# Transposes of k and q as row halves side by side, one exp per pair of heads, and a new order at both ends of the attention stage

## The chip, the cores and the metric

The kernel runs on one core of one Trainium2 chip. The metric is device time in microseconds (us), lower is better. PE is TensorE (its weight loads are listed as PEld), DVE is VectorE, ACT is ScalarE, POOL is GpSimd, SP is SyncE, which issues nearly all DMAs of this kernel.

## The reference

Attention with a soft cap on the scores, then two feed-forward stages on the 896 tokens that it gives:

```python
# q, k, v: (2, 12, 448, 64) f32, cap = 30
scores = cap * tanh(q @ k.T / sqrt(64) / cap)
attn = softmax(scores) @ v                       # then heads side by side: x (896, 768)
h = x @ w_in                                     # (896, 1024)
solu = h * softmax(h)
x = layer_norm(solu) * g_ln @ w_out              # (896, 768)
g, val = x @ w_gate, x @ w_val                   # (896, 1536) each
return (silu(g) * val) @ w_out2                  # (896, 768)
```

The weights arrive as 64-bit floats and are turned into f32 on the chip.

## The kernel before, in words

**Precision.** Every large product is made of three matmuls in the type float32r: a tensor is split into a high part (`hi_act`, `hi_dve`: a rounding copy on ACT or DVE) and a low part (`lo_dve`: the difference, on DVE), and hi·hi, hi·lo and lo·hi are added up in PSUM.

**Attention.** The 24 heads go two at a time, as 12 pairs; pair i has the tiles `k_i`, `q_i` and `v_i`. `attn_load` brings each of them with two DMAs, one per head: 448 rows of 64 numbers, laid out as 112 partitions that hold four consecutive rows each. `attn_T` transposes k and q of a pair on PE, 4 + 4 transposes of 112 rows x 128 columns into the PSUM tile `T` (tag `t`, two banks), and splits the result into `ks` (high part on ACT, for pair 1 on DVE; low part on DVE). `attn_qk(i, c)` makes chunk c of the scores, with 112 keys on the partitions: six matmuls into the PSUM tile `sc`, of which there are two (`psc`, bufs=2), head 0 from partitions 0 to 63 and head 1 from 64 to 127; ACT then takes the tanh of both heads (112x896) into `P`. `attn_exp` is an exp over two chunks at once (112x1792), so there are two per pair. `attn_sums` adds `P` up over the keys with matmuls against ones (tile `S`); DVE transposes the sums, POOL copies pieces of them, and `attn_recip` makes the reciprocals. `attn_pv` is the product with v (tile `pv`); `attn_norm` scales it and splits it into x.

**Order.** `attn_pair(i)` writes out the order by hand, and `InOrder` keeps it on each engine: while scores of pair i are made, k and q of pair i+1 are transposed, and sums, `pv` and norm of pair i-1 are done. `w_steps[i]` are four pieces of the conversion of `w_in` (tiles `wi`), which fill DVE. The 13th call, `attn_pair(12)`, has only the rest of pair 11 left, and takes three of the six steps of `h` for the first 128 tokens (`fill`) ahead of it; each step is six matmuls of 512 columns. `keep_warm(n)` issues n matmuls of zeros, 64x64, whose result nobody reads.

**After attention** the scheduler places instructions: h for seven blocks of 128 tokens, its softmax and layer norm, transposes (`lt`), x2, the gated stage and `ff2_out`, which writes 14 blocks of 128 x 384 results.

**Order of tokens.** Because a partition holds four consecutive rows of q, chunk c of a transposed q holds the rows 4p + c. The tokens stay in that order through both feed-forward stages, and `ff2_out` puts them right when it writes: each block goes out in two parts, the larger from SP's queue, the other from ACT's.

The functions that the diff touches, and what calls them:

Of the kernel before, what the change touches and what calls it, by code (L numbers as in the profile page):

```python
# [5 lines left out]
F32 = mybir.dt.float32  # L6
# [3 lines left out]
AF = mybir.ActivationFunctionType  # L10
# [26 lines left out]
class Kernel:  # L37
# [142 lines left out]
    def attn_load(self, i, names="kqv"):  # L180

        nc, CP = self.nc, self.CP
        b, p = divmod(i, self.NP)
        r = self.raws.setdefault(i, {})
        for n in names:
            src, bufs = {"k": (self.k, 2), "q": (self.q, 2), "v": (self.v, 3)}[n]
            r[n] = t = self.raw.tile([CP, 512], F32, name=f"{n}_{i}", tag=n, bufs=bufs)
            for j in range(2):
                sj = src[b, 2 * p + j].rearrange("(p c) d -> p c d", c=4)
                nc.sync.dma_start(t.rearrange("p (c h d) -> p c h d", c=4, h=2)[:, :, j, :], sj)  # L190

    def attn_T(self, i):

        CP, S = self.CP, self.S
        r = self.raws[i]
        ks = r["ks"] = self.at.tile([128, 2, 2, S], F32R, name=f"ks_{i}", tag="ks", bufs=2)
        ps = self.pt.tile([128, 2, 512], F32, name=f"T_{i}", tag="t")
        lots = ("k", "q") if i == 0 else ("kq",)
        for names in lots:
            for n in names:  # L200
                m = "kq".index(n)
                for c in range(4):
                    self.transpose(ps[:, m, c * CP:(c + 1) * CP], r[n][:, c * 128:(c + 1) * 128], self.ident[:CP, :CP])
            m = slice("kq".index(names[0]), "kq".index(names[-1]) + 1)
            (self.hi_dve if i == 1 else self.hi_act)(ks[:, m, 0], ps[:, m, :S])
            self.lo_dve(ks[:, m, 1], ps[:, m, :S], ks[:, m, 0])

    def attn_qk(self, i, c):


        CP, S = self.CP, self.S
        r = self.raws[i]
        ks = r["ks"]
        if c % 2 == 0:
            r["P", c // 2] = self.at.tile([CP, 2, 2, S], F32, name=f"P_{i}_{c}", tag="P", bufs=4)
        sc = self.psc.tile([128, 2, 512], F32, name=f"sc_{i}_{c}", tag="sc")
        for n, (u, w) in enumerate(((0, 0), (0, 1), (1, 0))):
            for j in range(2):
                h = slice(64 * j, 64 * j + 64)
                self.PE.matmul(sc[:CP, j, :S], ks[h, 0, u, c * CP:(c + 1) * CP], ks[h, 1, w, :], start=n == 0, stop=n == 2)  # L220
        self.A.activation(r["P", c // 2][:, c % 2], sc[:CP, :, :S], AF.Tanh, scale=self.c1[:CP])

    def attn_exp(self, i, g):


        P = self.raws[i]["P", g]
        self.A.activation(P, P, AF.Exp, scale=self.cp[:self.CP])

    def attn_sums(self, i):


        S = self.S
        r = self.raws[i]
        ps = self.pt.tile([128, 512], F32, name=f"S_{i}", tag="S")
        for m in range(2):
            for g in range(4):
                self.PE.matmul(ps[32 * g:32 * g + 32, :S], self.ones, r["P", m][:, g % 2, g // 2, :], start=m == 0,
                               stop=m == 1, tile_position=(0, 32 * g))
        tr = r["r"] = self.at.tile([128, S], F32, name=f"tr_{i}", tag="rc", bufs=2)
        sm = r["sm"] = self.at.tile([128, 32], F32, name=f"sm_{i}", tag="sm", bufs=2)[:, :S // 32]  # L240
        self.V.transpose(tr, ps[:, :S])
        for g in range(4):
            a, z = slice(32 * g, 32 * g + 32), slice(32 * (g ^ 1), 32 * (g ^ 1) + 32)
            self.G.tensor_copy(sm[a], tr[z, ::32])
# [9 lines left out]
    def attn_pv(self, i, c):  # L254

        S = self.S
        r = self.raws[i]
        if c == 0:
            r["pv"] = self.pt.tile([128, 512], F32, name=f"pv_{i}", tag="pv", bufs=1)
        for g in range(4):  # L260
            o = c * 128 + 32 * g
            self.PE.matmul(r["pv"][32 * g:32 * g + 32, :S], r["v"][:, o:o + 32], r["P", c // 2][:, c % 2, g // 2, :],
                           start=(c == 0), stop=(c == 3), tile_position=(0, 32 * g))

    def attn_norm(self, i):
# [10 lines left out]
    def attn_pair(self, i, fill=()):  # L276


        last, n = i - 1, 2 * self.NP
        if i == 0:  # L280
            self.attn_load(2, "v")
            self.w_in_load(1)
        elif i + 2 < n:
            self.attn_load(i + 2)
        w = self.w_steps[i]

        early = i > 1
        w[0]()
        if i < n:
            self.attn_qk(i, 0)  # L290
            self.attn_qk(i, 1)
        if i + 1 < n:
            self.attn_T(i + 1)
        if i < n:
            self.attn_exp(i, 0)
            if early:
                self.attn_qk(i, 2)
                self.attn_qk(i, 3)
        for f in fill:
            f()  # L300
        if i:
            self.attn_sums(last)
        w[1]()
        w[2]()
        if i:
            self.attn_pv(last, 0)
            self.attn_pv(last, 1)
            self.attn_recip(last)
        w[3]()
        if i < n:  # L310
            if not early:
                self.attn_qk(i, 2)
                self.attn_qk(i, 3)
            self.attn_exp(i, 1)
        if i:
            self.attn_pv(last, 2)
            self.attn_pv(last, 3)
            self.attn_norm(last)
# [174 lines left out]
            self.lo_dve(d[:, 1, :], f[:, m], d[:, 0, :])  # L493

    def ff2_out(self, half, t):
        nc, S, CP = self.nc, self.S, self.CP
        N = self.DM // 2
        acc = self.pt.tile([128, 512], F32, name=f"o_{half}_{t}", tag="m")[:, :N]
        for fc in range(self.K2):
            a, w = self.a[fc], self.w2[half, fc]  # L500
            c = slice(t * 128, (t + 1) * 128)
            self.mm3(acc, (a[:, 0, c], a[:, 1, c]), (w[:, 0, :], w[:, 1, :]), fc == 0, fc == self.K2 - 1)
        ob = self.slot("e", [128, N], f"ob_{half}_{t}", F32, bufs=2)
        nc.scalar.activation(ob, acc, AF.Copy)  # L504
        ov = self.out.rearrange("(b p c) e -> b c p e", b=self.B, c=4)
        r, parts = 0, []
        while r < 128:
            b, m = divmod(t * 128 + r, S)
            cc, p0 = divmod(m, CP)
            n = min(128 - r, CP - p0)  # L510
            parts.append((n, ov[b, cc, p0:p0 + n, half * N:(half + 1) * N], ob[r:r + n, :]))
            r += n
        for m, (_, dst, src) in enumerate(sorted(parts, key=lambda v: -v[0])):
            (nc.scalar if m else nc.sync).dma_start(dst, src)


    def run(self):
        nc = self.nc
# [6 lines left out]
        self.at = self.pool("at", side="right")  # L525
        psc = self.psc = self.pool("psc", bufs=2, space=PSUM)
        ptA = self.pt = self.ph = self.pool("ptA", bufs=1, space=PSUM)
        self.attn_load(0, "kq")
        self.setup()
        self.attn_load(1, "kq")  # L530
        self.wi = [self.slot(f"wi{u}", [128, KD, F1], f"wi{u}") for u in range(2)]
# [3 lines left out]
        w = [self.w_in_steps(i) for i in range(2 * KD)]  # L535
        none = lambda: None
        w = [(none,) * 4] + w + [(none,) * 4]
        self.w_steps = [(w[i][1], w[i][2], w[i + 1][0], w[i][3]) for i in range(2 * KD + 1)]
        self.attn_T(0)
        self.keep_warm(4)  # L540
        self.attn_load(0, "v")
        self.attn_load(2, "kq")
        self.w_in_load(0)
        self.attn_load(1, "v")
        nc.sync.dma_start(self.gt, self.g_ln.rearrange("(f p) -> p f", p=128))
        h = [self.ff1_h(t) for t in range(7)]
        for i in range(2 * self.NP):
            self.attn_pair(i)
        self.htag = "t"
        self.attn_pair(2 * self.NP, [f for _, f in h[0][:3]])  # L550
        for _, f in h[0][3:]:
            f()
        self.in_order = False
        self.at.release()
# [110 lines left out]
```

## Time and profile before

| | us |
|---|---|
| median of 3 runs | 503.4 (503.26 to 503.74) |
| the profiled execution, its own time | 504.33 |
| span in its profile, first to last instruction | 502.0 |
| PE busy | 492.1 (98%) |
| DVE busy | 351.9 (70%) |
| ACT busy | 251.1 (50%) |

The span is what the trace shows; the 2.3 us between it and the profiled execution's own time lie outside the instructions. The shares are means over stages that differ: attention takes the first 117 us of the span, and there ACT and DVE are far busier than their shares say.

### The profile page before, as it was taken

What the parts mean: (1) busy time and instruction counts of PE and PEld (TensorE: products, weight loads), DVE (VectorE), ACT (ScalarE), POOL (GpSimd) and SP (SyncE); (2) the same over time, 40 slices, a digit from 0 to 9 for tenths busy, and PEclk for the clock granted to TensorE, in tenths of its full rate; (3) what the DMA queues carried; (4) which work ended last, traced back from release to release, by engine and by line L of the source; (5) the groups of instructions that cost most, each with busy time, mean ns of one, the idle gap of its engine ahead of it and who ended that gap; (6) DMA issues with size and microseconds to landing.
All of it is one profiled execution on the core that took longest, in us unless ns stands there. A gap on an engine that the chain in (4) does not pass through costs nothing.

```text
span 502.0 us, 7647 instructions
## 1 busy us (share of the span) xinstructions
PE 492.1 (98%) x3016; PEld 406.1 (81%) x3016; DVE 351.9 (70%) x633; ACT 251.1 (50%) x373; POOL 21.9 (4%) x62
## 2 busy tenths in 40 slices
PE   7899999999999999999999999999999999999996
PEld 6454545456788899898899998889999989999996
DVE  2689999984778894769899999788997867200000
ACT  4999999961224695666544454444434434100000
POOL 1112121210000010000000000000000000000000
PEclk9899999999999999999999999999999999999999
DMA  6856564311000222243535445446344525111111
GB/s 146 218 130 165 129 164 117 103 44 42 1 0 23 76 73 85 85 146 128 185 127 164 151 144 172 125 127 188 96 126 104 179 64 157 33 33 31 33 31 31
DMA packets 66916, 52.40 MB, mean 104 GB/s; under 512 B 35904, under 2 KB 62272, under 8 KB 66880
## 3 DMA queue, kind: packets, MB, share of 16 engines
q1 hardware_dynamic: 66112, 51.13, 35.3%
q10 hardware_dynamic: 736, 0.79, 0.4%
q8 instruction: 23, 0.38, 0.3%
q14 instruction: 13, 0.11, 0.1%
q0 software_dynamic: 32, 0.00, 0.0%
HBM read 49.16 MB, written 2.75 MB: 103 GB/s over the span
## 4 chain that ended last, share of the span: by engine, by line
PE 94%; ACT 3%; DVE 2%; issue 0%; POOL 0%; POOLq 0%
PE o L29 17%; PE g L29 17%; PE v L29 17%; PE x L29 11%; PE h L29 10%; PE pv L29 7%; PE sc L29 6%; PE S L29 4%; PE T L29 2%; ACT P L29 2%; PE lt L29 1%; DVE sm L29 1%; PE warm L29 1%; DVE e L29 0%; ACT e L29 0%
## 5 line engine op out<-in xcount | busy, mean ns | idle before, releaser
L29 PE MATMUL g<-x,y 128*128 128x512 f32 (+1 forms) x432 | 91.2, 363 | 0.0
L29 PE MATMUL v<-x,y 128*128 128x512 f32 (+1 forms) x432 | 90.5, 362 | 0.0
L29 PEld LDWEIGHTS g<-x,y 128*128 128x128 f32 x432 | 78.5, 188 | 8.9
L29 PEld LDWEIGHTS v<-x,y 128*128 128x128 f32 x432 | 78.2, 188 | 8.5
L29 PE MATMUL h<-wi,x 128*128 128x512 f32 x252 | 58.9, 392 | 0.0
L29 PEld LDWEIGHTS h<-wi,x 128*128 128x128 f32 x252 | 46.9, 188 | 11.0 <-issue 1.5
L29 PE MATMUL o<-x,a 128*128 128x384 f32 x294 | 52.3, 334 | 0.0
L29 PEld LDWEIGHTS o<-x,a 128*128 128x128 f32 x294 | 51.1, 188 | 0.0
L29 ACT ACTIVATE P<-sc,consts 112x896 f32<-112x896 f32 x48 | 45.8, 1009 | 5.7 <-PE sc L29 5.7
L29 ACT ACTIVATE P<-P,consts 112x1792 f32<-112x1792 f32 x24 | 43.0, 1794 | 0.5
L29 PE MATMUL sc<-ks 64*112 64x448 f32 x288 | 37.0, 385 | 2.7 <-ACT P L29 2.4
L504 ACT ACTIVATE ob<-o 128x384 f32<-128x384 f32 x14 | 6.9, 492 | 64.0 <-PE o L29 64.0
L29 PE MATMUL pv<-P,v 112*32 112x448 f32 x384 | 38.5, 539 | 0.0
L29 PE MATMUL x<-lB,wo 128*128 128x256 f32 (+1 forms) x192 | 37.3, 338 | 0.4 <-ACT lB L29 0.4
L29 PEld LDWEIGHTS sc<-ks 64*112 64x112 f32 x288 | 23.3, 174 | 17.3 <-issue 6.6
L29 PE MATMUL o<-y,a 128*128 128x384 f32 x189 | 34.1, 334 | 0.0
L29 PEld LDWEIGHTS x<-lB,wo 128*128 128x128 f32 x192 | 30.1, 189 | 3.6 <-ACT lB L29 0.6
L29 PEld LDWEIGHTS o<-y,a 128*128 128x128 f32 x189 | 32.9, 188 | 0.1
L29 PEld LDWEIGHTS pv<-P,v 112*32 112x32 f32 x384 | 12.3, 110 | 23.5 <-issue 23.2
L29 PE MATMUL x<-lA,wo 128*128 128x384 f32 x144 | 28.5, 336 | 0.0
L29 PEld LDWEIGHTS x<-lA,wo 128*128 128x128 f32 x144 | 25.1, 188 | 1.1
L29 DVE SCALAR_TENSOR_TENSOR w<-w_raw,w 128x768 uint32<-128x768 uint32 (+1 forms) x26 | 23.1, 891 | 0.3
(90 smaller groups left out, 628.1 us busy)
## 6 DMA issues: line engine op xcount, KB each, us to landing
wg_raw<-in_moe_w_gate_dram SPq DMA_DIRECT2D x12, 768.0 KB, 4.2
wv_raw<-in_moe_w_val_dram SPq DMA_DIRECT2D x12, 768.0 KB, 4.2
w_raw<-in_moe_w_out_dram SPq DMA_DIRECT2D x11, 768.0 KB, 4.5
wi_raw<-in_moe_w_in_dram SPq DMA_DIRECT2D x12, 512.0 KB, 4.7
wo_raw<-in_moe_w_out_dram SPq DMA_DIRECT2D x12, 512.0 KB, 3.4
k<-in_k_dram SPq DMA_DIRECT2D x24, 112.0 KB, 2.9
q<-in_q_dram SPq DMA_DIRECT2D x24, 112.0 KB, 4.0
v<-in_v_dram SPq DMA_DIRECT2D x24, 112.0 KB, 2.9
```

What stands on the lines that cost most here:

```text
L29: i = f(*a, **k)
L504: nc.scalar.activation(ob, acc, AF.Copy)
```

## The change

- k and q of a pair share one tile `kq` of 128 partitions: k on partitions 0 to 63, q on 64 to 127, seven chunks of 64 rows each, in natural order. Each still comes with two DMAs, now 64 partitions x 7 rows. v keeps 112 partitions, with rows in natural order.
- `attn_T` makes 14 transposes of 64 rows x 128 columns per pair, alternately k (rows 0 to 63 of PE's array) and q (rows 64 to 127), into different PSUM banks.
- For pair 0, q is loaded and transposed first, into the bank of tag `S`; k follows into the bank of tag `t`, and its split is made in two pieces: the first chunk's 112 columns, then the other 336. Two `keep_warm` matmuls lie between, 14 behind the transposes of pair 1, and the four of before are gone.
- `P` is one tile per pair, and one exp covers its four chunks (112x3584).
- In each `attn_pair`, chunks 2 and 3 of the scores now come before the exp, right behind the transposes. In pair 0 all four chunks come before the transposes of pair 1. In the last pair the first step of h stands between chunks 1 and 2; the other five follow pair 11's `pv`.
- Tokens are in natural order everywhere, so each block of results goes out with one DMA from SP's queue.

```diff
         for n in names:
-            src, bufs = {"k": (self.k, 2), "q": (self.q, 2), "v": (self.v, 3)}[n]
-            r[n] = t = self.raw.tile([CP, 512], F32, name=f"{n}_{i}", tag=n, bufs=bufs)
+            if n == "v":
+                r[n] = t = self.raw.tile([CP, 512], F32, name=f"v_{i}", tag="v", bufs=3)
+                src, a = self.v, CP
+            else:
+                if "kq" not in r:
+                    r["kq"] = self.raw.tile([128, 896], F32, name=f"kq_{i}", tag="kq", bufs=2)
+                t = r["kq"][64 * "kq".index(n):][:64]
+                src, a = {"k": self.k, "q": self.q}[n], 64
             for j in range(2):
-                sj = src[b, 2 * p + j].rearrange("(p c) d -> p c d", c=4)
-                nc.sync.dma_start(t.rearrange("p (c h d) -> p c h d", c=4, h=2)[:, :, j, :], sj)
+                sj = src[b, 2 * p + j].rearrange("(c p) d -> p c d", p=a)
+                nc.sync.dma_start(t.rearrange("p (c h d) -> p c h d", h=2, d=64)[:, :, j, :], sj)
...
-        ps = self.pt.tile([128, 2, 512], F32, name=f"T_{i}", tag="t")
-        lots = ("k", "q") if i == 0 else ("kq",)
-        for names in lots:
-            for n in names:
-                m = "kq".index(n)
-                for c in range(4):
-                    self.transpose(ps[:, m, c * CP:(c + 1) * CP], r[n][:, c * 128:(c + 1) * 128], self.ident[:CP, :CP])
+        if i:
+            ps = self.pt.tile([128, 2, 512], F32, name=f"T_{i}", tag="t")
+            lots = [(ps, "kq", S)]
+        else:
+            ps = [self.pt.tile([128, 512], F32, name=f"T_{n}", tag=t) for n, t in (("q", "S"), ("k", "t"))]
+            lots = [(p.unsqueeze(1), n, w) for p, n, w in zip(ps, "qk", (S, CP))]
+        for ps, names, w in lots:
+            for c in range(7):
+                for j, n in enumerate(names):
+                    a = slice(0, 64) if n == "k" else slice(64, 128)
+                    self.transpose(ps[:, j, c * 64:(c + 1) * 64], r["kq"][a, c * 128:(c + 1) * 128], self.ident[a, a])
             m = slice("kq".index(names[0]), "kq".index(names[-1]) + 1)
-            (self.hi_dve if i == 1 else self.hi_act)(ks[:, m, 0], ps[:, m, :S])
-            self.lo_dve(ks[:, m, 1], ps[:, m, :S], ks[:, m, 0])
+            for a in (slice(0, w), slice(w, S)):
+                if a.start < a.stop:
+                    (self.hi_dve if i == 1 else self.hi_act)(ks[:, m, 0, a], ps[:, :, a])
+                    self.lo_dve(ks[:, m, 1, a], ps[:, :, a], ks[:, m, 0, a])
+            if names == "q":
+                self.keep_warm(2)
...
-        early = i > 1
         w[0]()
         if i < n:
             self.attn_qk(i, 0)
             self.attn_qk(i, 1)
+        if i == 0:
+            self.attn_qk(i, 2)
+            self.attn_qk(i, 3)
         if i + 1 < n:
             self.attn_T(i + 1)
-        if i < n:
-            self.attn_exp(i, 0)
-            if early:
-                self.attn_qk(i, 2)
-                self.attn_qk(i, 3)
+        if i == 0:
+            self.keep_warm(14)
         for f in fill:
             f()
+        if 0 < i < n:
+            self.attn_qk(i, 2)
+            self.attn_qk(i, 3)
+        if i < n:
+            self.attn_exp(i)
         if i:
             self.attn_sums(last)
...
-        if i < n:
-            if not early:
-                self.attn_qk(i, 2)
-                self.attn_qk(i, 3)
-            self.attn_exp(i, 1)
...
-        ov = self.out.rearrange("(b p c) e -> b c p e", b=self.B, c=4)
...
-        for m, (_, dst, src) in enumerate(sorted(parts, key=lambda v: -v[0])):
-            (nc.scalar if m else nc.sync).dma_start(dst, src)
+        nc.sync.dma_start(self.out[t * 128:(t + 1) * 128, half * N:(half + 1) * N], ob)
...
+        self.htag = "t"
         for i in range(2 * self.NP):
-            self.attn_pair(i)
-        self.htag = "t"
-        self.attn_pair(2 * self.NP, [f for _, f in h[0][:3]])
-        for _, f in h[0][3:]:
+            self.attn_pair(i, [f for _, f in h[0][:1]] if i == 2 * self.NP - 1 else ())
+        self.attn_pair(2 * self.NP)
+        for _, f in h[0][1:]:
             f()
```

The first place is PE's queue at the start. A row is a run of matmuls with their output and inputs; `T` is a tile of transposes, `sc_c` the scores of chunk c, and buffer numbers tell the pairs apart. Before:

```order
L29 MATMUL T_129<-ident,k_73 128x112 x4
L29 MATMUL T_129<-ident,q_76 128x112 x4
L29 MATMUL warm<-z 64x64 x4
L29 MATMUL sc_0_168<-ks_128 112x448 x6
L29 MATMUL sc_1_176<-ks_128 112x448 x6
L29 MATMUL T_185<-ident,k_119 128x112 x4
L29 MATMUL T_185<-ident,q_122 128x112 x4
L29 MATMUL sc_2_204<-ks_128 112x448 x6
L29 MATMUL sc_3_212<-ks_128 112x448 x6
L29 MATMUL sc_0_233<-ks_184 112x448 x6
```

And the same place in the changed kernel:

```order
L29 MATMUL T_q<-ident,kq_73 128x64 x7
L29 MATMUL warm<-z 64x64 x2
L29 MATMUL T_k<-ident,kq_73 128x64 x7
L29 MATMUL sc_0_172<-ks_126 112x448 x6
L29 MATMUL sc_1_180<-ks_126 112x448 x6
L29 MATMUL sc_2_188<-ks_126 112x448 x6
L29 MATMUL sc_3_196<-ks_126 112x448 x6
L29 MATMUL T_205<-ident,kq_118 128x64 x14
L29 MATMUL warm<-z 64x64 x14
L29 MATMUL sc_0_255<-ks_204 112x448 x6
```

Pair 0's q now precedes its k, its four chunks stand together, and pair 1's transposes come behind them.

The second place is PE's queue at the last pair, from its first chunk to the sums of pair 11 (`h` is the first step of the feed-forward). Before:

```order
L29 MATMUL sc_0_1283<-ks_1203 112x448 x6
L29 MATMUL sc_1_1291<-ks_1203 112x448 x6
L29 MATMUL sc_2_1301<-ks_1203 112x448 x6
L29 MATMUL sc_3_1309<-ks_1203 112x448 x6
L29 MATMUL S_1317<-P_0_1186,ones 32x448 x4
L29 MATMUL S_1317<-P_2_1216,ones 32x448 x4
L29 MATMUL pv_1338<-P_0_1186,v_976 32x448 x8
L29 MATMUL pv_1338<-P_2_1216,v_976 32x448 x8
L29 MATMUL h_1366<-wi_125,x 128x512 x2
```

In the changed kernel:

```order
L29 MATMUL sc_0_1337<-ks_1253 112x448 x6
L29 MATMUL sc_1_1345<-ks_1253 112x448 x6
L29 MATMUL h_1353<-wi_123,x 128x512 x2
L29 MATMUL h_1353<-wi_124,x 128x512 x2
L29 MATMUL h_1353<-wi_123,x 128x512 x2
L29 MATMUL sc_2_1360<-ks_1253 112x448 x6
L29 MATMUL sc_3_1368<-ks_1253 112x448 x6
L29 MATMUL S_1377<-P_1236,ones 32x448 x8
L29 MATMUL pv_1398<-P_1236,v_1019 32x448 x16
L29 MATMUL S_1425<-P_1336,ones 32x448 x8
```

One step of h has moved between chunks 1 and 2, and the sums of pair 11 follow pair 10's `pv` with nothing between.

The third place is ACT's queue in one pair (the transposes' split is `ks<-T`, the tanh `P<-sc`, the exp `P<-P`). Before:

```order
L29 ACTIVATE P_0_339<-sc_0_340,consts 112x896
L29 ACTIVATE P_0_339<-sc_1_348,consts 112x896
L29 ACTIVATE ks_356<-T_357 128x2x448
L29 ACTIVATE P_0_339<-P_0_339,consts 112x1792
L29 ACTIVATE P_2_369<-sc_2_370,consts 112x896
L29 ACTIVATE P_2_369<-sc_3_378,consts 112x896
L29 ACTIVATE P_2_369<-P_2_369,consts 112x1792
```

In the changed kernel:

```order
L29 ACTIVATE P_364<-sc_0_365,consts 112x896
L29 ACTIVATE P_364<-sc_1_373,consts 112x896
L29 ACTIVATE ks_381<-T_382 128x2x448
L29 ACTIVATE P_364<-sc_2_399,consts 112x896
L29 ACTIVATE P_364<-sc_3_407,consts 112x896
L29 ACTIVATE P_364<-P_364,consts 112x3584
```

The first exp has gone from behind the split, and one exp of twice the size closes the pair.

## Rows read from the trace of the kernel before

**Rows 1.** Busy time by stretch: start:end, us, engines, granted clock, DMA share, GB/s.

```profile
14.98:18.39 3.41, 3.41 (x18) 2.32 (x22) 2.64 (x5) 3.41 (x3) 0.00 (x0) 0.53 0.78 207
33.12:100.11 66.99, 66.99 (x645) 33.37 (x641) 61.74 (x120) 63.93 (x57) 11.18 (x32) 1.00 0.52 133
117.37:497.00 379.63, 378.74 (x1993) 347.16 (x1990) 259.10 (x449) 153.72 (x286) 4.22 (x7) 1.00 0.31 96
```

**Rows 2.** Timeline of PE over one pair in mid-attention: start, us, instruction.

```profile
33.12 1.48 PE L29 MATMUL sc<-ks 64*112 64x448 f32 x12
34.53 0.60 PE L29 MATMUL T<-ident,k 112*128 112x112 f32 x4
...
35.44 1.47 PE L29 MATMUL sc<-ks 64*112 64x448 f32 x12
...
41.49 1.47 PE L29 MATMUL sc<-ks 64*112 64x448 f32 x12
```

**Rows 3.** Timeline of ACT over the same pair; in brackets idle time before, and releaser.

```profile
34.03 1.91 ACT L29 ACTIVATE P<-sc,consts 112x896 f32<-112x896 f32 x2 [0.30 <-PE sc L29]
35.82 0.92 ACT L29 ACTIVATE ks<-T 128x896 fp32r<-128x896 f32 x1
36.62 1.79 ACT L29 ACTIVATE P<-P,consts 112x1792 f32<-112x1792 f32 x1
...
42.40 1.91 ACT L29 ACTIVATE P<-sc,consts 112x896 f32<-112x896 f32 x2 [0.35 <-PE sc L29]
```

**Rows 4.** Timeline of DVE: pair 1's low part; then its one wait in mid-attention.

```profile
12.00 1.09 DVE L29 TENSOR_TENSOR ks<-T,ks 128x896 fp32r<-128x896 f32 x1
...
38.62 0.65 DVE L29 STREAM_TRANSPOSE tr<-S 128x448 f32<-128x448 f32 x1 [0.32 <-PE S L29]
```

**Rows 5.** Timeline of PE from the last pair's first chunk to the feed-forward.

```profile
100.11 1.48 PE L29 MATMUL sc<-ks 64*112 64x448 f32 x12
102.08 1.75 PE L29 MATMUL sc<-ks 64*112 64x448 f32 x12 [0.49 <-ACT P L29]
103.75 1.71 PE L29 MATMUL S<-P,ones 112*32 112x448 f32 x16
...
108.40 4.39 PE L29 MATMUL h<-wi,x 128*128 128x512 f32 x18
...
117.37 12.58 PE L29 MATMUL h<-wi,x 128*128 128x512 f32 x54
```

**Rows 6.** Timeline of PE at the start.

```profile
4.90 0.57 PE L29 MATMUL T<-ident,k 112*128 112x112 f32 x4
6.76 0.60 PE L29 MATMUL T<-ident,q 112*128 112x112 f32 x4 [1.29 <-DVE ks L29]
...
14.04 2.36 PE L29 MATMUL sc<-ks 64*112 64x448 f32 x12 [1.79 <-ACT P L29]
...
24.23 1.47 PE L29 MATMUL sc<-ks 64*112 64x448 f32 x12
```

**Rows 7.** Timeline of ACT at the start.

```profile
7.40 0.54 ACT L29 ACTIVATE ks<-T 128x448 fp32r<-128x448 f32 x1 [1.35 <-PE T L29]
9.36 1.91 ACT L29 ACTIVATE P<-sc,consts 112x896 f32<-112x896 f32 x2 [1.41 <-PE sc L29]
...
16.62 1.89 ACT L29 ACTIVATE P<-sc,consts 112x896 f32<-112x896 f32 x2
```

**Rows 8.** Timeline of SP's DMA queue at the start: when the loads are issued.

```profile
0.74 1.40 SPq L190 DMA_DIRECT2D k<-in_k_dram  x2
2.17 1.29 SPq L190 DMA_DIRECT2D q<-in_q_dram  x2
```

**Rows 9.** DMA issues: the largest part of a block of results, us to landing.

```profile
out_dram<-ob SPq DMA_DIRECT2D x4, 168.0 KB, 2.2
```

**Rows 10.** Timeline of PE's weight loads for one pair's transposes.

```profile
34.52 0.39 PEld L29 LDWEIGHTS T<-ident,k 112*128 112x128 f32 x4 [0.33 <-issue]
34.87 0.43 PEld L29 LDWEIGHTS T<-ident,q 112*128 112x128 f32 x4
```

More of the change, by code (lines that the diff above doesn't have):

```diff
@@ L213, in attn_qk @@
         ks = r["ks"]
-        if c % 2 == 0:
-            r["P", c // 2] = self.at.tile([CP, 2, 2, S], F32, name=f"P_{i}_{c}", tag="P", bufs=4)
+        if c == 0:
+            r["P"] = self.at.tile([CP, 4, 2, S], F32, name=f"P_{i}", tag="P", bufs=2)
         sc = self.psc.tile([128, 2, 512], F32, name=f"sc_{i}_{c}", tag="sc")
@@ L220, in attn_qk, with attn_exp @@
                 self.PE.matmul(sc[:CP, j, :S], ks[h, 0, u, c * CP:(c + 1) * CP], ks[h, 1, w, :], start=n == 0, stop=n == 2)
-        self.A.activation(r["P", c // 2][:, c % 2], sc[:CP, :, :S], AF.Tanh, scale=self.c1[:CP])
-    def attn_exp(self, i, g):
-        P = self.raws[i]["P", g]
+        self.A.activation(r["P"][:, c], sc[:CP, :, :S], AF.Tanh, scale=self.c1[:CP])
+    def attn_exp(self, i):
+        P = self.raws[i]["P"]
         self.A.activation(P, P, AF.Exp, scale=self.cp[:self.CP])
@@ L236, in attn_sums @@
             for g in range(4):
-                self.PE.matmul(ps[32 * g:32 * g + 32, :S], self.ones, r["P", m][:, g % 2, g // 2, :], start=m == 0,
+                self.PE.matmul(ps[32 * g:32 * g + 32, :S], self.ones, r["P"][:, 2 * m + g % 2, g // 2, :], start=m == 0,
                                stop=m == 1, tile_position=(0, 32 * g))
@@ L261, in attn_pv @@
             o = c * 128 + 32 * g
-            self.PE.matmul(r["pv"][32 * g:32 * g + 32, :S], r["v"][:, o:o + 32], r["P", c // 2][:, c % 2, g // 2, :],
+            self.PE.matmul(r["pv"][32 * g:32 * g + 32, :S], r["v"][:, o:o + 32], r["P"][:, c, g // 2, :],
                            start=(c == 0), stop=(c == 3), tile_position=(0, 32 * g))
@@ L495, in ff2_out @@
     def ff2_out(self, half, t):
-        nc, S, CP = self.nc, self.S, self.CP
+        nc = self.nc
         N = self.DM // 2
@@ L504, in ff2_out @@
         nc.scalar.activation(ob, acc, AF.Copy)
-        ov = self.out.rearrange("(b p c) e -> b c p e", b=self.B, c=4)
[L506 to L512, printed above, removed]
-        for m, (_, dst, src) in enumerate(sorted(parts, key=lambda v: -v[0])):
-            (nc.scalar if m else nc.sync).dma_start(dst, src)
+        nc.sync.dma_start(self.out[t * 128:(t + 1) * 128, half * N:(half + 1) * N], ob)
     def run(self):
@@ L527, in run @@
         ptA = self.pt = self.ph = self.pool("ptA", bufs=1, space=PSUM)
-        self.attn_load(0, "kq")
+        self.attn_load(0, "qk")
         self.setup()
@@ L539, in run @@
         self.attn_T(0)
-        self.keep_warm(4)
         self.attn_load(0, "v")
```

## The prediction

> **What bounds the kernel now.** I began with busy time by stretch. From 33.12 to 100.11 us PE is busy in all of 66.99 us, and after 117.37 us in 378.74 of 379.63 [rows 1]. So what PE gets rid of by 117 us shortens the run, as long as no other engine comes late, and what other engines get rid of is worth nothing by itself.
>
> Then PE's timeline over one pair [rows 2]: the first chunks of two pairs stand at 33.12 and 41.49, a period of 8.37 us. It holds chunks 0 and 1 (1.41, to 34.53), the transposes (0.91, to 35.44), and chunks 2 and 3, sums and `pv` (6.05). ACT waits 0.35 us for scores in it [rows 3], so it needs about 8.02; DVE waits 0.32 for the sums [rows 4], so it needs about 8.05. Both are close behind PE.
>
> The most telling place is the last pair, which has no transposes [rows 5]. It still takes 8.29 us (100.11 to 108.40), although PE has 0.91 less to do. Chunk 2 starts at 102.08, 1.97 after chunk 0 and not 1.41, because it needs one of the two `sc` tiles back: it waits 0.49 for ACT's tanh of chunk 0. Chunk 3 waits likewise for the tanh of chunk 1, inside the same row, which takes 1.75 where 1.47 is usual. So transposes that get shorter soon only uncover this wait.
>
> At the start PE's second set of transposes waits 1.29 us for DVE [rows 6], since k and q of pair 0 share one `T`; ACT has its first tanh at 9.36 [rows 7]. PE then idles 1.79 us ahead of 14.04 [rows 6], and right after it, from 14.98 to 18.39, the granted clock is at the lower level, 1.2 of 2.4 GHz (0.53 over the stretch) [rows 1].
>
> **The transposes in mid-attention.** Now eight of 112 columns take 0.91 us, the first four 0.44, so 0.11 each [rows 2]. The new 14 have 64 columns. No row shows such a transpose; one costs between 64/112 of 0.11, which is 0.063, and 0.11. One after another that is 0.88 to 1.54 per pair, two at a time 0.44 to 0.77. That row halves work at once the scores show: 12 matmuls of 64 rows and 448 columns take 1.41 us [rows 2], 0.117 each, while h's 54 of 512 columns take 12.58 [rows 5], 0.233 each, or 0.204 scaled to 448. I take seven turns of 0.063 and 0.1 to get going, about 0.55, because the scores are the nearest rows in form. Then chunk 2 could start 1.96 us after chunk 0, just where the tanh lets it, and the pair takes what the last one takes, 8.29. The saving is 0.08 a pair and 0.64 over the eight periods from 33.12 to 100.11. DVE (8.05) and ACT follow.
>
> **One exp per pair.** ACT's copy of 448 columns takes 0.54 us [rows 7], of 896 0.92 [rows 3], so a further column costs 0.85 ns. An exp of 3584 is then 1.79 + 1792 x 0.85 ns = 3.3 us, 0.2 to 0.3 less than two [rows 3]. Nothing waits for ACT in mid-attention but chunks 2 and 3, which wait for tanhs that stand where they stood; so I count nothing here. The sums need the exp later than it is done: it ends about 0.4 us into the next pair, and the sums come 3.64 into it [rows 5]. The two tanhs now ahead of it find their scores ready.
>
> **The start.** k's loads leave SP's queue by 2.14 us [rows 8] and its transposes start at 4.90 [rows 6], 2.76 later; q's leave at 3.46, so q is there at about 6.22. With the order turned round, q is transposed at 4.90 (seven turns, 0.44 to 0.77) and split before k comes at 6.22. k takes 0.44 to 6.66, some 0.25 us pass until ACT starts (before, 0.64 from the first transpose to the split, 6.76 to 7.40 [rows 6, 7]), and 112 columns take 0.54 - 336 x 0.85 ns = 0.25. Chunk 0 starts at 7.25, and its tanh 0.91 later, as from 33.12 to 34.03 [rows 2, 3]: 8.16 instead of 9.36.
>
> ACT then sets the pace. Chunk 2 of pair 0 waits for the first tanh (9.2), its own tanh comes 0.91 later at 10.1, and the exp follows two tanhs of 1.91 together [rows 3], at about 12.05. With 3.3 us of exp, less 0.1 by which ACT's instructions overlap (34.03 + 1.91 against 35.82 [rows 3]), pair 1's first tanh is at 15.25 instead of 16.62 [rows 7]. Pair 1's scores are ready by then: its transposes end at about 11.3, DVE's two halves of the split take 1.09 each [rows 4] (I take the first to be as long as the second), to 13.8. The 14 matmuls of zeros lie within that wait and cost nothing; were it gone, they would cost up to 1.7 us (28 passes of 0.063).
>
> From a pair's first tanh to its sums it is 2.73 us where PE waits for ACT (103.75 - 100.11 - 0.91), and sums and `pv` take 4.65 (to 108.40) [rows 5]. So pair 2's first chunk comes at 15.25 + 2.73 + 4.65 = 22.63 instead of 24.23 [rows 6]: 1.60 gained. The next period was 8.89 (24.23 to 33.12 [rows 2, 6]) and becomes 8.29: 0.60.
>
> **The last pair.** From its first chunk to the point where three of six steps of h and all of attention are done it was 17.26 us (100.11 to 117.37 [rows 5]). A step of h is 12.58/9 = 1.40. Now: chunks 0 and 1 to 1.41, the step to 2.81, chunks 2 and 3 to 4.25, pair 10's sums and `pv` to 8.90. ACT starts the tanh of chunk 2 at 3.72 and the exp at 5.65, which ends at 8.95; pair 11's sums start at about 9.05, `pv` ends at 13.70, two more steps at 16.50. Gained: 0.76. The step fills PE's two waits for the tanhs.
>
> **Loads, results, the rest.** There are as many loads as before, of the same 112 KB, issued at the same pace; in mid-attention they run two pairs ahead. One DMA of 192 KB per block replaces two; the largest part lands 2.2 us after issue [rows 9], and 24 KB more may move the last landing by 0.2 us either way. ACT's issues that fall away lie in a stage where PE alone sets the end. I count nothing for all of it.
>
> **The sum.** 1.60 + 0.60 + 0.64 + 0.76 = 3.6 us. The profiled execution took 504.33 with a span of 502.0; its span would become 498.4. It stands 0.9 above the median of 503.4, so the timed runs should show 503.4 - 3.6 = **499.8**. About 0.2% (1 us) is what a measurement here can tell from no change.
>
> **The rivals.**
> *A, the loads of 64 partitions come later.* At the start two loads are issued per 1.29 us [rows 8], and everything hangs on the second tensor. If each took twice the pace, k would be complete 1.3 us later, with the whole start: 501.1. For it speaks that the transfers are dense there, 207 GB/s at a DMA share of 0.78 [rows 1]; against it that issuing, not moving, spaces the first loads. The Trainium skill (SBUF — State Buffer, section Door 1: The DMA port swizzle) says that partitions 0 to 63 reach only eight of 16 ports, about 196 GB/s for 1 MiB. By that the first loads (112 KB per 0.65 us, 176 GB/s) would pass and the stretch at 207 GB/s would not quite; I keep the issue pace for the sum.
> *B, the lower clock stays.* PE still waits for pair 1's first tanh around 15 to 16 us. If the clock falls as before for 3.4 us, some 2.3 us of PE's work there take twice as long and ACT's waits hide about half: 1.2 lost, 501.0. Against it stand the zeros, which fill most of the gap that came before the fall.
> *C, the 14 transposes run one after another at 0.063.* The block is then as long as now (0.88): 0.08 in each of nine periods is not gained, and some 0.3 at the start: 500.8.
> *D, on the other side: they run one after another and each costs what one costs now.* The block is 1.54, the period 9.00. Against 8.29 that is 0.71 in each of nine periods, 6.4, and 0.5 at the start: 503.4 - 3.6 + 6.9 = 506.7. It decides once the block is over about 1.23 us: 0.83 is where the period passes 8.29 (8.37 - 0.91 + 0.83), and 0.4 more in nine periods eat the 3.6. Against it speak the scores' halves and the weight loads: four of 128 columns start within 0.35 us (34.52 to 34.87), 0.087 each [rows 10].
> The Trainium skill (TensorE: Matmul & The Clock Gate, section LDWEIGHTS) would bring D about: it gives columns/1.2 ns for a weight load whatever the rows, 107 ns for 128 columns, 1.49 us for 14 in a row and a time near 506. The 0.087 is below that, so at the full clock the trace does not bear it out.
> *E, nothing is gained*, because a wait that no row shows takes the place of those removed: within 1 us of 503.4.
>
> **How the numbers follow.** The forecast has 0.64, A 0.12, B 0.10, C 0.06, D 0.04, E 0.04. The forecast's own range, 499.1 to 500.5, comes from the bounds of the single-file transposes at the start (0.3), the results (0.2) and the clock; with A to C it is 498.7 to 501.6. Faster: forecast, A, B, C, less 0.01 for two of these together, 0.91. Same: E, 0.04. Slower: D and that 0.01, 0.05.
>
> **What would show it.** Right: the first tanh near 8.2 us, pair 2's first chunk near 22.6, a period of 8.29 with PE waiting some tenths for ACT ahead of chunk 2 or 3, transposes of about 0.5 per pair, pair 11's sums about 9 us behind its first chunk, no stretch at the lower clock near 15 us. Wrong: a period above 8.37, transposes above 0.95, PE waiting for a load of `kq`, or DVE falling behind so that `pv` or the scores wait for it.

## The result: 0.85% slower, and the profile after

The changed kernel took 507.8 us (median of 6 runs, 507.05 to 508.92) beside 503.4 of the kernel before on the same chip (6 runs): a ratio of 1.0085, 95% interval 1.0069 to 1.0101. 499.8 was predicted, with 501.6 as the upper end. The profiled execution took 507.78 with a span of 506.0.

**Attention went nearly as predicted.** PE's timeline of the changed kernel at the start, over one period and at the last pair answers to [rows 2, 5, 6]:

```profile
5.02 1.01 PE L29 MATMUL T_q<-ident,kq 64*128 64x64 f32 x7
6.58 0.64 PE L29 MATMUL T_k<-ident,kq 64*128 64x64 f32 x7
...
23.00 1.48 PE L29 MATMUL sc<-ks 64*112 64x448 f32 x12
...
31.32 1.48 PE L29 MATMUL sc<-ks 64*112 64x448 f32 x12
32.62 0.60 PE L29 MATMUL T<-ident,kq 64*128 64x64 f32 x14
33.29 1.76 PE L29 MATMUL sc<-ks 64*112 64x448 f32 x12
...
39.63 1.47 PE L29 MATMUL sc<-ks 64*112 64x448 f32 x12
...
97.82 1.48 PE L29 MATMUL sc<-ks 64*112 64x448 f32 x12
99.22 1.66 PE L29 MATMUL h<-wi,x 128*128 128x512 f32 x6
...
107.00 1.71 PE L29 MATMUL S<-P,ones 112*32 112x448 f32 x16
...
111.84 7.34 PE L29 MATMUL h<-wi,x 128*128 128x512 f32 x31
124.67 10.45 PE L29 MATMUL h<-wi,x 128*128 128x512 f32 x35 [5.49 <-DVE e L29]
134.96 1.03 PE L29 MATMUL lt<-ident,e 128*128 128x128 f32 x8
```

Pair 2's first chunk stands at 23.00 (24.23 before), the period is 8.31 (39.63 - 31.32; 8.37 before), and the point that was at 117.37 before, three of block 0's six steps of h done, is at 111.84 + 2 x 1.40 = 114.64. So the changed kernel leads by 2.73 us there. ACT's timeline at the start answers to [rows 7]: the first tanh, and pair 1's, which was at 16.62.

```profile
8.48 3.89 ACT L29 ACTIVATE P<-sc,consts 112x896 f32<-112x896 f32 x4 [0.17 <-PE sc L29]
...
15.60 1.88 ACT L29 ACTIVATE P<-sc,consts 112x896 f32<-112x896 f32 x2
```

**Then it loses 7.2.** The row at 124.67 is new: PE stands 5.49 us for DVE. In the kernel before, PE's timeline runs on from [rows 5] to the first transposes after h with one wait of 0.53:

```profile
130.47 1.09 PE L29 MATMUL lt<-ident,e 128*128 128x128 f32 x8 [0.53 <-DVE e L29]
```

From the equal points it is 13.10 us to `lt` before (130.47 - 117.37) and 20.32 after (134.96 - 114.64). DVE's timeline of the changed kernel shows what is waited for: the last read of block 0's h.

```profile
122.49 0.75 DVE L29 SCALAR_TENSOR_TENSOR e<-e,sm,h 128x512 f32<-128x512 f32 x1
...
123.88 0.73 DVE L29 SCALAR_TENSOR_TENSOR e<-e,sm,h 128x512 f32<-128x512 f32 x1
```

And the stretches of the changed kernel around it (columns as in [rows 1]: the seventh entry is the granted clock):

```profile
119.20:124.67 5.47, 0.00 (x1) 0.00 (x1) 3.78 (x9) 1.45 (x4) 0.00 (x0) 0.81 0.00 0
122.90:129.70 6.80, 5.03 (x12) 3.99 (x13) 3.76 (x8) 0.00 (x0) 0.56 (x1) 0.52 0.00 0
```

PE is idle in the first; in the second the granted clock is 0.52, that is the lower of the two levels (1.2 of 2.4 GHz) nearly throughout, and the matmuls that follow the idle stretch run at it. The 35 of them take 10.29 us (124.67 to 134.96); at the 0.233 each of before [rows 5] they would take 8.15. So the stall costs its 5.49 and the lower clock 2.1 more. The wait of 0.53 ahead of `lt` is gone, which leaves 7.1 of the 7.2. After it both kernels take nearly the same: 371.0 us from `lt` to the end of the span (506.0 - 134.96), 371.5 before (502.0 - 130.47).

**Why block 1's h waits for block 0's.** The program's PSUM tiles lie on banks 0 to 7. The program's allocator gives the tags of a pool their banks in the order in which they are first claimed, and the pool `pm`, opened behind attention for h's blocks 1 to 6, goes round all eight. Where the program puts the tiles:

```
tile                       before    after
sc (psc, two tiles)        0-1, 2-3  0-1, 2-3
tag pv (zeros, pv)         4         4
tag t (T; then h block 0)  5-6       6-7
tag S                      7         5
h block 1 (pm, two tiles)  0 and 7   0 and 7
```

The change transposes q of pair 0 into a tile with tag `S` and only then claims `T_k` with tag `t`. That moves `t` up by one, and with it block 0's h, which keeps that tag: its second half now lies on bank 7, where block 1's second tile will be. Before, that tile waited for pair 11's sums, long done; now it waits for DVE's softmax of block 0.

### The profile page after: what moved, and what is told of

The parts are those of the page before. It is cut to its first block, busy times and chain, and to the rows that moved or that the text cites. A ratio compares the mean times of both kernels' runs of the same rounds, so it can differ in the third digit from the quotient of the medians.

```text
span 506.0 us, 7801 instructions
## 1 busy us (share of the span) xinstructions
PE 493.0 (97%) x3112; PEld 406.6 (80%) x3112; DVE 352.3 (70%) x634; ACT 248.7 (49%) x362; POOL 21.8 (4%) x62
## 4 chain that ended last, share of the span: by engine, by line
PE 93%; ACT 5%; DVE 1%; issue 0%; ACTq 0%
PE o L29 17%; PE g L29 17%; PE v L29 17%; PE h L29 12%; PE x L29 11%; PE pv L29 7%; PE sc L29 6%; ACT P L29 4%; PE S L29 4%; PE lt L29 1%; PE warm L29 1%; DVE sm L29 1%; ACT e L29 0%; DVE e L29 0%; ACT wo L29 0%
## 5 line engine op out<-in xcount | busy, mean ns | idle before, releaser
L29 PE MATMUL h<-wi,x 128*128 128x512 f32 x252 | 61.3, 403 | 5.5 <-DVE e L29 5.5
L29 PEld LDWEIGHTS h<-wi,x 128*128 128x128 f32 x252 | 48.4, 194 | 17.0 <-DVE e L29 5.9
L29 PE MATMUL sc<-ks 64*112 64x448 f32 x288 | 38.8, 387 | 2.5 <-ACT P L29 1.1
L29 ACT ACTIVATE P<-P,consts 112x3584 f32<-112x3584 f32 x12 | 39.5, 3289 | 0.4
```

The source lines that it names most:

```text
L29: i = f(*a, **k)
```

## The experiments

They were made in three lots, each beside runs of the kernel before (medians 503.6, 503.8 and 503.9); differences of a few tenths between lots show nothing. In the first three the theory is the bank.

**Undo the bank alone.** The changed kernel with `T_k` claimed first; transposes, order and all else stay.

```diff
-            ps = [self.pt.tile([128, 512], F32, name=f"T_{n}", tag=t) for n, t in (("q", "S"), ("k", "t"))]
-            lots = [(p.unsqueeze(1), n, w) for p, n, w in zip(ps, "qk", (S, CP))]
+            ps = [self.pt.tile([128, 512], F32, name=f"T_{n}", tag=t) for n, t in (("k", "t"), ("q", "S"))]
+            lots = [(p.unsqueeze(1), n, w) for p, n, w in zip(ps[::-1], "qk", (S, CP))]
```

> The changed kernel with one line altered: the tile for pair 0's k is claimed ahead of that for q, so that PSUM banks go as in the kernel before (T and block 0's h on banks 5 and 6, S on 7). Nothing else changes. Theory 1 (banks): block 1's second h tile, which always gets bank 7, no longer waits for DVE's last read of block 0's h; the 5.49 us wait of PE and the stretch at the lower clock behind it go, 7.0 us in all (the lead of 2.7 us at 112 us became a lag of 4.3 at 134.7 us), so about 500.7 us, 2.7 below the kernel before. Theory 2 (order): block 0's softmax came late because h's first step was moved and its five others run in one piece; then the bank makes no difference and it stays near 507.8.

Measured: 500.2 us, ratio 0.9932 (0.9919 to 0.9945). In PE's timeline the wait is gone:

```profile
111.41 15.26 PE L29 MATMUL h<-wi,x 128*128 128x512 f32 x66
127.19 1.09 PE L29 MATMUL lt<-ident,e 128*128 128x128 f32 x8 [0.53 <-DVE e L29]
```

One line of allocation is worth 7.6 us. The new order of h is not the cause.

**Put the bank into the kernel before.** One matmul of zeros of the warm-up goes into a tile with tag `S`, so that `S` is claimed ahead of `t`; nothing else changes.

```diff
-        self.keep_warm(18)
+        self.keep_warm(17)
+        ps = self.pt.tile([128, 512], F32, name="first", tag="S")
+        self.PE.matmul(ps[:64, :64], self.z, self.z, start=True, stop=True)
```

> The kernel before, with one of its 18 first matmuls of zeros written into the tile of tag S, so that S is claimed ahead of T and the banks go as in the changed kernel (S on 5, T and block 0's h on 6 and 7). Theory 1 (banks): the same wait of about 5.5 us appears behind block 0's h, with a fall of the clock, so 503.4 + 7.0 = 510.4 us (508.9 if the clock holds). Theory 2 (order): no change, 503.4.

Measured: 512.8 us, ratio 1.0166 (1.0146 to 1.0187). PE's timeline has the same wait:

```profile
117.88 4.64 PE L29 MATMUL h<-wi,x 128*128 128x512 f32 x19
128.01 10.54 PE L29 MATMUL h<-wi,x 128*128 128x512 f32 x35 [5.49 <-DVE e L29]
138.39 1.04 PE L29 MATMUL lt<-ident,e 128*128 128x128 f32 x8
```

From 117.88 to `lt` it is 20.51 us, 7.41 over the 13.10 of before. With the 0.5 lost ahead of 117.88 (117.37 before) that makes up the difference of the two profiles (spans of 509.8 and 502.0). The medians differ by more, 9.2: two of the four executions had spans of 511.1 at a mean granted clock of 0.985, where the profiled one had 0.992. Where their clock was lower no trace shows. The collision needs nothing of the change but the order of claims.

**Zeros in the stall.** 44 matmuls of zeros behind block 0's h in the changed kernel, to part the wait from the clock.

```diff
+        self.keep_warm(44)
```

> The changed kernel, with 44 matmuls of zeros (88 passes of 0.058 us, 5.1 us) put behind block 0's h, inside the wait for bank 7; the bank stays as it is. Theory 1 has two parts, the wait (5.5 us) and the lower clock after it (1.5 us). If the idle time of PE lowered the clock, the zeros keep it up and the time falls by about 1.5 us, to 506.3. If the lower clock cost nothing, or comes anyway, it stays at 507.8.

Measured: 505.5 us, ratio 1.0040 (1.0026 to 1.0054), 2.2 below the changed kernel. PE's timeline, and then the stretch, at full clock:

```profile
119.29 5.35 PE L29 MATMUL warm<-z 128*64 128x64 f32 x88
124.57 8.79 PE L29 MATMUL h<-wi,x 128*128 128x512 f32 x36
133.19 1.03 PE L29 MATMUL lt<-ident,e 128*128 128x128 f32 x8
```

```profile
119.30:126.00 6.70, 6.69 (x94) 6.16 (x94) 4.87 (x10) 1.45 (x4) 0.00 (x0) 1.00 0.01 2
```

The wait is still there under the zeros; what they give back is the clock, 2.2 by the medians. I had reckoned 1.5, because I had not counted the wait of 0.53 that is gone. The traces agree with the medians: behind the stall 36 matmuls of h take 8.62 us here (124.57 to 133.19), where 35 took 10.29.

From here on every kernel is built on the one with the bank undone (500.2), to size the prediction's terms.

**Two exps again**, in the place of the one.

```diff
-        self.A.activation(P, P, AF.Exp, scale=self.cp[:self.CP])
+        for g in range(2):
+            p = P[:, 2 * g:2 * g + 2]
+            self.A.activation(p, p, AF.Exp, scale=self.cp[:self.CP])
```

> As e1_bank, with the one exp of 112x3584 cut into two of 112x1792 in the same place. The prediction counts nothing for the merged exp: within 0.3 us of e1_bank, although ACT has 0.2 to 0.3 us more to do in each of 12 pairs. Rival (ACT sets the pair's pace since chunks 2 and 3 wait for its tanhs): 2.4 to 3.6 us above e1_bank.

Measured: 500.05 us, ratio 0.9931 (0.9916 to 0.9946). The one exp is worth nothing that shows here.

**The old transposes**: k and q in tiles of 112 partitions, eight transposes a pair.

```diff
...
-            for c in range(7):
-                for j, n in enumerate(names):
-                    a = slice(0, 64) if n == "k" else slice(64, 128)
-                    self.transpose(ps[:, j, c * 64:(c + 1) * 64], r["kq"][a, c * 128:(c + 1) * 128], self.ident[a, a])
+            for j, n in enumerate(names):
+                for c in range(4):
+                    self.transpose(ps[:, j, c * CP:(c + 1) * CP], r[n][:, c * 128:(c + 1) * 128], self.ident[:CP, :CP])
```

> The changed kernel with k's tile T of pair 0 claimed ahead of q's (500.2 us), but with the eight transposes of 112 rows by 128 columns of the kernel before in place of the 14 in row halves, and k and q in tiles of 112 partitions again. Theory: PE's block of transposes goes from 0.60-0.66 back to 0.91 us in each of ten pairs, but the two waits of PE for the tanhs (0.20 and 0.43 a pair) swallow most of it: the period goes from 8.31 to 8.37, 0.5 us in nine periods, and the start moves by at most 0.3: 500.5 to 501.0. Rival: the row halves (or their loads) are worth their whole 0.3 us in each of ten pairs: 503.

Measured: 500.1 us, ratio 0.9930 (0.9917 to 0.9943). The period is 8.38 in its trace, and the last pair's first chunk stands at 97.98 and not 97.38; the median does not show these 0.6. The row halves, the loads with them, are worth 0.6 us by the profiles here, and nothing by the medians.

**No step of h among the last pair's chunks**: three steps ahead of pair 11's sums again.

```diff
-            self.attn_pair(i, [f for _, f in h[0][:1]] if i == 2 * self.NP - 1 else ())
-        self.attn_pair(2 * self.NP)
-        for _, f in h[0][1:]:
+            self.attn_pair(i)
+        self.attn_pair(2 * self.NP, [f for _, f in h[0][:3]])
+        for _, f in h[0][3:]:
```

> The changed kernel with k's tile T of pair 0 claimed ahead of q's (500.2 us), but with no step of h among the last pair's chunks: the first three steps stand ahead of pair 11's sums, as in the kernel before. Theory: the last pair takes 17.26 us to the point where it took 16.82 (102.08 and 103.75 show PE's two waits for the tanhs that the step fills), so 0.4 more, up to the 0.76 that the prediction gave: 500.6 to 501.0. Rival: the step only moves a wait to pair 11's sums, which wait 0.86 for the exp: 500.2.

Measured: 500.7 us, ratio 0.9944 (0.9929 to 0.9960), 0.45 more, as the theory has it. In the profiles the last pair takes 17.27 us to three steps done, and 16.83 with the early step.

**No zeros behind pair 1's transposes.**

```diff
-            self.keep_warm(14)
+            pass
```

> The changed kernel with k's tile T of pair 0 claimed ahead of q's (500.2 us), without the 14 matmuls of zeros behind pair 1's transposes. If PE's idle time there lowers its clock, as it did in the kernel before (0.53 from 14.98 to 18.39 us), the scores and transposes of pairs 1 and 2 run at half pace and the time is 0.5 to 1.5 longer: 500.7 to 501.7 (the prediction's rival B gave 1.2). If not, the zeros do nothing: 500.2.

Measured: 500.7 us, ratio 0.9951 (0.9935 to 0.9968). This is inconclusive: six of its ten runs lie at 499.9 to 500.8 and four at 502.8 to 503.0, and the profiled one, of the first kind, waits 1.28 us at that place with a granted clock of 1.00. No trace shows one of the four. Kernels that have the zeros also have such runs, one of six with two exps (502.3) and one of six without the early step (502.9).

**The start undone**: k of pair 0 first, both in one tile, one split each, chunks 2 and 3 behind pair 1's transposes, zeros as before.

```diff
-            ps = [self.pt.tile([128, 512], F32, name=f"T_{n}", tag=t) for n, t in (("k", "t"), ("q", "S"))]
-            lots = [(p.unsqueeze(1), n, w) for p, n, w in zip(ps[::-1], "qk", (S, CP))]
+            ps = self.pt.tile([128, 2, 512], F32, name=f"T_{i}", tag="t")
+            lots = [(ps[:, m:m + 1], n, S) for m, n in enumerate("kq")]
...
-        if i == 0:
-            self.attn_qk(i, 2)
-            self.attn_qk(i, 3)
...
-            self.keep_warm(14)
...
-        if 0 < i < n:
+        if i < n:
...
-        self.attn_load(0, "qk")
+        self.attn_load(0, "kq")
...
+        self.keep_warm(4)
```

> The changed kernel with k's tile T of pair 0 claimed ahead of q's (500.2 us), with the start of the kernel before: k of pair 0 loaded and transposed first, q into the other half of the same tile, each split in one piece, chunks 2 and 3 of pair 0 behind the transposes of pair 1, four matmuls of zeros behind those of pair 0 and none later. Theory (the start gives 1.6 to 2.2 of the prediction's 3.6): pair 1's first tanh moves from about 15.2 to 16.6, the time to 501.4 to 502.2. Rival: the start is worth nothing that lasts, 500.2 to 500.6.

Measured: 504.5 us, ratio 1.0011 (1.0001 to 1.0021): the new start is worth 4.3 us, over twice the 1.2 to 2.0 that I had expected. PE's timeline, and then two stretches:

```profile
18.32 2.58 PE L29 MATMUL sc<-ks 64*112 64x448 f32 x12 [2.85 <-ACT P L29]
20.83 3.21 PE L29 MATMUL S<-P,ones 112*32 112x448 f32 x16
...
27.34 1.47 PE L29 MATMUL sc<-ks 64*112 64x448 f32 x12
```

```profile
8.00:11.00 3.00, 3.00 (x22) 2.29 (x22) 0.62 (x1) 1.05 (x2) 0.00 (x0) 0.50 0.93 255
...
18.00:23.00 5.00, 4.68 (x24) 2.26 (x28) 1.09 (x1) 4.89 (x6) 0.00 (x0) 0.50 0.94 233
```

Pair 1's first tanh is at 17.28 and not 15.20, which is 2.1. From there to pair 2's first chunk it takes 10.06 us and not 7.39, another 2.7: PE idles 2.85 for ACT, whose one long exp of pair 0 now stands ahead of pair 1's tanhs, and then runs at the lower clock. Pair 2's first chunk comes at 27.34, and in the kernel before, whose start has two exps, at 24.23 [rows 6]. That the one exp makes the difference is read from PE's wait and was not tested by itself.

**Half of the sums into PE's wait.** The first eight matmuls of pair i-1's sums go between the transposes and chunk 2 of pair i; `attn_sums` takes the half as its second argument.

```diff
...
+        if i:
+            self.attn_sums(last, 0)
         if 0 < i < n:
             self.attn_qk(i, 2)
...
-            self.attn_sums(last)
+            self.attn_sums(last, 1)
```

> The changed kernel with k's tile T of pair 0 claimed ahead of q's (500.2 us), and with the first half of the sums of pair i-1 (eight matmuls, 0.76 us) between the transposes and chunks 2 and 3 of pair i. Theory: PE is then no longer held by the two waits for the tanhs (0.20 and 0.43 a pair), and the period falls from 8.31 to what DVE needs, 8.31 less its wait of 0.25 for the sums, 8.06: 0.25 in nine periods, 2.2 us: 498.0 to 498.6. Rival: chunk 2's tanh comes later by the 0.1 us that PE runs past it, the exp and the next pair's tanhs follow, and ACT becomes the bound with nothing gained: 500.2 or more.

Measured: 497.9 us, ratio 0.9886 (0.9871 to 0.9902), with a period of 8.03 (8.06 expected). The theory held: DVE, which waited 0.25 us a pair for the sums, has no wait for them in this trace.

**The same with the old transposes.**

> The kernel with half of the sums in the wait (497.9 us; period 8.03), with the eight transposes of 112 rows in place of the 14 in row halves, which cost nothing while PE waited for the tanhs (500.1 against 500.2). Theory: PE has no wait left there, so the block's 0.33 us (0.84 from the first transpose to the next matmul against 0.52) now lengthens each period from 8.03 to about 8.36: 2.6 in nine periods less what falls at the ends: 500.0 to 500.6. Rival: ACT or DVE is what sets 8.03, PE has as much to spare as before: 497.9 to 498.2.

Measured: 502.6 us, ratio 0.9969 (0.9957 to 0.9980): 4.8 more by the medians, not 2.6. PE's timeline with the row halves, then with the old transposes:

```profile
40.06 1.48 PE L29 MATMUL sc<-ks 64*112 64x448 f32 x12
41.37 0.59 PE L29 MATMUL T<-ident,kq 64*128 64x64 f32 x14
41.90 0.96 PE L29 MATMUL S<-P,ones 112*32 112x448 f32 x8
...
48.09 1.48 PE L29 MATMUL sc<-ks 64*112 64x448 f32 x12
```

```profile
39.94 1.47 PE L29 MATMUL sc<-ks 64*112 64x448 f32 x12
41.34 0.60 PE L29 MATMUL T<-ident,k 112*128 112x112 f32 x4
41.78 0.55 PE L29 MATMUL T<-ident,q 112*128 112x112 f32 x4
42.26 0.96 PE L29 MATMUL S<-P,ones 112*32 112x448 f32 x8
...
48.44 1.48 PE L29 MATMUL sc<-ks 64*112 64x448 f32 x12
```

From the first chunk to the sums it takes 1.84 (41.90 - 40.06) and 2.32: 0.48 a pair, of which 0.39 is the block itself (0.53 and 0.92) and 0.09 the change from scores to transposes. The whole period is 8.03 (48.09 - 40.06) and 8.50 (48.44 - 39.94), which makes 4.2 in nine periods; the rest of the 4.8 is not traced. The ratios to the kernel before differ by 0.0083, which is 4.2 us as well. The same transposes that were worth 0.6 or nothing while PE waited are worth nearly 1% of the run once it doesn't.

**The same with two exps.**

> The kernel with half of the sums in the wait (497.9 us; period 8.03, no wait left in ACT's row), with the exp of each pair cut in two. Two exps of 112x1792 take 3.58 us where one of 112x3584 takes 3.29. Theory: ACT is as full as PE there, so the period grows by up to 0.29, to 8.3: 2.3 to 2.6 more in eight to nine periods: 500.0 to 500.5. Rival: ACT has slack that its row does not show, as in the kernel where the cut cost nothing (500.05 against 500.22): 497.9 to 498.2.

Measured: 496.9 us, ratio 0.9855 (0.9840 to 0.9870), the fastest of all. My theory fell: the period is 8.04 with two exps and 8.03 with one. ACT's timeline with two, then with one:

```profile
42.00 1.91 ACT L29 ACTIVATE P<-sc,consts 112x896 f32<-112x896 f32 x2
43.80 3.47 ACT L29 ACTIVATE P<-P,consts 112x1792 f32<-112x1792 f32 x2
47.31 1.90 ACT L29 ACTIVATE P<-sc,consts 112x896 f32<-112x896 f32 x2
```

```profile
43.69 1.91 ACT L29 ACTIVATE P<-sc,consts 112x896 f32<-112x896 f32 x2
45.63 3.29 ACT L29 ACTIVATE P<-P,consts 112x3584 f32<-112x3584 f32 x1
49.00 1.91 ACT L29 ACTIVATE P<-sc,consts 112x896 f32<-112x896 f32 x2
```

From the tanhs of chunks 2 and 3 to the next pair's tanh it is 5.31 us in both (47.31 - 42.00, 49.00 - 43.69): the one exp is 0.18 shorter, but starts 1.94 after those tanhs and not 1.80. At the last pair, two are better: pair 11's sums can begin when its first exp is done, and PE's wait of 0.81 ahead of them goes. That accounts for some 0.5 of the 1.0 between the medians; the two were timed in different lots, and the runs with one exp spread from 497.3 to 499.7.

## Why the prediction was wrong

**The step that failed** is the one in "What bounds the kernel now" and "Loads, results, the rest": that what PE gets rid of by 117 us shortens the run, with nothing counted behind attention. I had taken PE's 378.74 busy of 379.63 us there [rows 1] as given, although the diff's line with `(("q", "S"), ("k", "t"))` changes which tag is claimed first, and with it the bank of block 0's h. What stood there in place of nothing was 5.49 us of wait and 2.1 us of matmuls slowed by the lower clock. Rival E ("a wait that no row shows") was its nearest name, at 0.04 and bounded at no gain; no rival had a wait that costs more than the change saves. D gave 506.7, but by slow transposes, and those were fast.

Its own steps, by the profile of the changed kernel, and by the experiments where these say more:

- **The start**, 1.60 predicted, 1.23 in this profile and 1.64 with the bank undone (22.59). The two executions differ by the pace of q's first seven transposes, 1.01 us here and 0.64 there; the trace's first record of the granted clock, at the full level, begins at 6.54 here and at 5.05 there. Pair 1's first tanh was forecast at 15.25 and came at 15.60, and at 15.20 there.
- **Pair 2's period**, 0.60 predicted, 0.57 measured (8.32 instead of 8.89).
- **Eight periods**, 0.64 predicted, 0.49 measured: 8.31 each (66.50 from 31.32 to 97.82), not 8.29. The transposes took what I had taken for them, 0.53 to 0.66 with 0.55 forecast, and PE's waits for the tanhs swallowed the rest. Rivals C and D fall with it. The Trainium skill (TensorE: Matmul & The Clock Gate, section LDWEIGHTS) gives columns/1.2 ns, by which I estimate 1.49 us for the 14 in a row; where nothing delays PE the trace has 0.53 for loads and transposes together (41.37 to 41.90), so the measurement decides against that rule for row halves at the full clock.
- **The last pair**, 0.76 predicted, 0.44 measured, and 0.45 by undoing the step. It was over-sized: pair 11's sums came 9.18 behind its first chunk (9.05 forecast), and its `pv` then waited 0.17 more for DVE to read the tile.
- **One exp**, nothing predicted, nothing measured. The reason, that PE waits only for the tanhs, was not the whole of it: even where ACT has no wait left, the exp's 0.18 us are lost on ACT itself by the later start (5.31 us with one exp and with two).
- **Loads, results, the rest**, nothing predicted. From `lt` to the end of the span it is 371.1 us with the bank undone (498.3 - 127.19) and 371.5 before. What makes the 0.4 was not tried.
- **A** did not happen: by it k would have come 1.3 us after the forecast 6.22, and its transposes start at 6.19 with the bank undone. **B** did not in this profile (granted clock 1.00 from its first record, at 6.54, to 22 us).

With the bank undone the sum was nearly met: 3.4 us by the medians (503.6 - 500.2) and 3.7 by the spans (502.0 - 498.3), 3.6 predicted. Part of that is luck: the periods and the last pair gave less than forecast, and the 0.4 behind `lt`, which nothing in the sum stands for, made up for it.

## What to carry to other kernels

Where a change claims a tile earlier or later, look up which banks every tag gets before and after, and which tile of a later pool lands on each: the cost can lie in a stage that the diff never touches. A saving on PE was worth next to nothing while PE waited for ACT, and its whole size once that wait was filled, so try the edits together with what fills the wait (here half of the sums) before dropping them. Undoing one line at a time on top of the repaired kernel sized the start, the last pair, the exp and the transposes; the total alone said only "slower".

## What was not expected of the hardware

- 5.5 us of PE idleness cost 2.1 to 2.2 us more through the granted clock, which fell to its lower level at 122.6 and stayed there for some 6.8 us; zeros in the idle stretch gave that back.
- At the start PE's pace differs between executions of the same instructions, and the column of the granted clock hides it. With two exps on the repaired kernel (this execution took 502.3) pair 0's 24 score matmuls run as

```profile
7.94 5.15 PE L29 MATMUL sc<-ks 64*112 64x448 f32 x24 [0.35 <-ACT ks L29]
```

  and with one exp the same 24 take 3.76 us from start to end (7.16 to 10.92). The rows run from q's transposes to pair 2's first chunk:

```profile
5.03 0.64 PE L29 MATMUL T_q<-ident,kq 64*128 64x64 f32 x7
...
7.16 1.79 PE L29 MATMUL sc<-ks 64*112 64x448 f32 x12 [0.35 <-ACT ks L29]
9.14 1.78 PE L29 MATMUL sc<-ks 64*112 64x448 f32 x12 [0.18 <-ACT P L29]
...
22.59 1.48 PE L29 MATMUL sc<-ks 64*112 64x448 f32 x12
```

  The column reads 1.00 in both, but it does so wherever the trace has no record of the clock. The first record, at the full level, begins at 13.69 us in the first execution and at 5.05 in the second. Ahead of 13.69 twelve scores take 2.58 (half of 5.15), as long as in the row at 18.32 above, in a stretch whose clock is 0.50. By that pace PE ran at the lower level up to there. Likewise q's seven transposes take 1.01 in the changed kernel, ahead of its first record at 6.54, and 0.64 here. With the zeros in the stall, whose start is that of the changed kernel, the clock had risen at 3.89 and fell again in this stretch:

```profile
8.00:11.00 3.00, 3.00 (x18) 1.90 (x18) 0.34 (x1) 2.10 (x3) 0.00 (x0) 0.55 0.74 168
```

  The late rise puts pair 2's first chunk 2.2 us later (24.80 and 22.59). That is the size by which some single runs lie above their median, though only the profiled executions can be read so. What sets the time of the rise was not tried.
